# Background matmuls of an attention stream, placed one at a time instead of two

## The chip, the core and the metric

The kernel runs on one core of a Trainium2 chip. The time is the device time in microseconds (us) of one execution; a run is repeated and the median is given. The engines are named as in the profile: PE is TensorE (its matmuls), PEld its weight loads, DVE is VectorE, ACT is ScalarE, POOL is GpSimd, SP is SyncE, which issues the DMAs here. Each engine works through its own queue in order, so an instruction that waits holds up everything behind it on that engine.

## The reference

Two transformer layers with the same weights: attention with 32 heads of 16 columns over 2048 tokens, then a dense layer with SiLU. Matrices are bfloat16.

```
def _A_ref(x, wqkv, wo):            # x: 2048 x 512, 32 heads of 16
    q, k, v = split_heads(x @ wqkv)
    p = softmax(q k^T / 4)          # 32 x 2048 x 2048
    return merge_heads(p @ v) @ wo
def _B_ref(x, w1, w2):              # 512 -> 1792 -> 512
    return silu(x @ w1) @ w2
for layer in range(2):
    x = x + _A_ref(layernorm(x), wqkv, wo)
    x = x + _B_ref(layernorm(x), w1, w2)
```

## The kernel before

**The stream.** The 2048 x 2048 scores of 32 heads and two layers are cut into blocks of 128 keys by 512 queries for one head: 4096 blocks. A batch (`t` in the main loop) holds four blocks. PE makes their scores in one group, since each score has only 32 contraction rows and four of them fit the array side by side (`score`, L852). ACT exponentiates three of the four blocks, in one instruction of 512 columns and one of 1024 (`exp`, L1083). DVE makes the fourth by writing the bits of a half-precision number directly (`emit_d`, `d_y`, L1001), and POOL derives two more terms of it (`d_z`). In every second batch, called a pv batch below (`t in pv_steps`), PE multiplies the exponentials of two batches with the values (`emit_pv`, `to_o`, L876). There are 1024 batches. The first ones, before the DVE path has started, give ACT all four blocks.

**The background.** Everything else of both layers is cut into parts and put between the batches: the projections to queries, keys, values and output (`proj_q`, `proj_k`, `proj_v`, `out_add`, all through `mm4`: four matmuls of 128 x 128 by 128 x 512 into one PSUM bank), the two dense products (`ffn`: `h_ps` by `mm4`, 14 times per block of 512 tokens, each followed by a tanh on ACT and a product on DVE, then four sums of 14 matmuls each in `f_ps`), the layer norms (`xn`), and the normalization of the heads (`rec`, `attn`, L601 and L603). A background product takes its PSUM bank from the pool `m`, which has one buffer once the first batches are over. The next group's first matmul therefore waits until DVE has read the last group out.

**The order** is fixed when the program is built. `Model` keeps an estimate of the time at which PE, ACT and DVE are done, and `part(...)` announces what the next piece of a background generator costs: `pe` for time on PE, `dve` for time on DVE. After the scores, values and exponentials of a batch are emitted, the main loop asks `bg.heads(t)` for candidates and takes one as long as `bg.fits(item)` says yes. For PE, `fits` wants the piece, the next scores and their way to ACT, and a margin of 0.1 us, to end before ACT's queue runs out:

```
        if pe:
            end = self.pe_end(pe, sums) + self.SWITCH
            return end + self.GROUP + self.TO_ACT + self.margin <= self.act
```

`SWITCH` (0.1 us) is charged when PE goes from one kind of matmul to another, `GROUP` (0.217 us) for a matmul of 512 columns or a group of four small ones side by side. When a result is needed at once, `bg.ensure` places its pieces without asking. When no background of PE was placed in a batch that is not a pv batch, `fill` adds three groups of multiplications with zeros, to keep PE busy. After the last batch what is left is emitted, and `tail` does the last block's output projection and dense layer on its own.

Of the kernel before, what the change touches and what calls it, by code (L numbers as in the profile page):

```python
# [24 lines left out]
def part(dve=0.0, pe=0.0, held=False, sums=False, need=None):  # L25

    return Part(held, pe, dve, sums, need)
# [191 lines left out]
def kernel(  # L219
# [19 lines left out]
    CT = D // P  # L239
    NC = S // 512  # L240
    FT = F // P
# [70 lines left out]
    def load_x(c, src=None, parts=1):  # L312
        x_sb[c] = xpool.tile([P, 4, D], BF16, name="x", tag="x")
        if src is None:
            src = xf[512 * c : 512 * (c + 1), :].rearrange("(tt p) d -> p tt d", p=P)
        n = 4 // parts
        for i in range(0, 4, n):
            nc.sync.dma_start(x_sb[c][:, i : i + n, :], src[:, i : i + n, :])
# [26 lines left out]
    bg = Background()  # L345
# [35 lines left out]
    def bank(name, dtype=FP32):  # L381
        home = "o" if early[0] and next(turn) % 2 else "m"
        shape = [P, 2048 // mybir.dt.size(dtype)]
        return psum[home].tile(shape, dtype, name=name, tag=home)[:]
# [34 lines left out]
    def ln_pair(c, i):  # L419

        stats[c, i] = yield from ln_stats(c, (i, i + 1))
# [26 lines left out]
    def ln_attn(L, c):  # L448
        xnT[L, c] = xslot((c, (c + 1) % 4)[L], "xnT")
        if L == 0 and c + 1 < NC:  # L450
            load_x(c + 1)
        yield from ln_chunk(c, xnT[L, c])
        if L == 0 and c + 1 == NC:
            load_x(0)
# [4 lines left out]

    def mm4(name, lhs, rhs, out=0.6):  # L460

        yield part(pe=0.43)
        ps = bank(name)
        for ct in range(CT):
            r = rhs(ct)
            nc.tensor.matmul(  # L466
                ps.rearrange("p (t q) -> p t q", q=P) if len(r.shape) == 3 else ps,
                lhsT=lhs(ct),
                rhs=r,
                start=(ct == 0),  # L470
                stop=(ct == CT - 1),
            )
            if ct == 1:
                yield part(pe=0.43, held=True)
        yield part(out, held=True)
        return ps

# [151 lines left out]
    def load_wo():  # L629

        wo[0] = hpool.tile([P, FT, 512], BF16, name="wo", tag="hT")
        nc.sync.dma_start(wo[0][:, 0:CT, :], A_wo.rearrange("(ct p) e -> p ct e", p=P))
# [15 lines left out]
    def silu_tanh(h_ps, t_sb):  # L648
        nc.scalar.activation(t_sb, h_ps, ACT.Tanh, scale=0.5)  # L649

    def silu_mul(ft, h_ps, t_sb, hT):
        nc.vector.scalar_tensor_tensor(  # L652
            out=hT[:, ft, :], in0=t_sb, scalar=1.0, in1=h_ps, op0=ALU.add, op1=ALU.mult
        )

    def ffn_out(L, c, i, y_ps):
        nc.vector.scalar_tensor_tensor(
            out=x_sb[c][:, i, :],
            in0=y_ps,
            scalar=0.5,  # L660
            in1=x_sb[c][:, i, :],
            op0=ALU.mult,
            op1=ALU.add,
        )
        tt = 4 * c + i
        nc.sync.dma_start(of[tt * P : (tt + 1) * P, :] if L == 1 else x1[c][:, i, :], x_sb[c][:, i, :])
# [23 lines left out]
    def ffn(L, c):  # L690
        if (L, c) != (1, NC - 1):
            nxt = (c + 1) % NC
            load_x(nxt, x1[nxt] if (L, c) >= (0, NC - 1) else None)
        w1 = W1()
        yield part(need=("fT", L, c))
        fT = fTs.pop((L, c))
        hT = hpool.tile([P, FT, 512], BF16, name="hT", tag="hT")
        for ft in range(FT):
            w = w1.get(ft)
            h_ps = yield from mm4(  # L700
                "h_ps", lambda ct: w[:, ct, :], lambda ct: fT[:, :, ct, :], out=0
            )
            t_sb = tpool.tile([P, 512], FP32, name="t_sb", tag="t")
            silu_tanh(h_ps, t_sb[:])
            yield part(0.6, held=True)
            silu_mul(ft, h_ps, t_sb[:], hT)
        for tq in range(4):
            yield part(pe=0.43)
            y_ps = bank("f_ps")
            for ft in range(FT):  # L710
                nc.tensor.matmul(  # L711
                    y_ps,
                    lhsT=hT[:, ft, tq * P : (tq + 1) * P],
                    rhs=w2_sb[:, ft, :],
                    start=(ft == 0),
                    stop=(ft == FT - 1),
                )
                if ft % 2 == 1 and ft < FT - 1:
                    yield part(pe=0.43, held=True)
            yield part(0.6, held=True)  # L720
            ffn_out(L, c, tq, y_ps)
            if L == 0 and tq % 2 == 1:
                bg.add_side(None, ln_pair(c, tq - 1))
        if L == 0:
            bg.add_side(("ln", 1, c), ln_attn(1, c))
        if (L, c) != (1, NC - 1):
            load_wo()
# [98 lines left out]
    steps, pv_steps = plan()  # L826
    pv_left = {}
    for ts in pv_steps.values():
        t, k = ts[0]
# [19 lines left out]
    def score(blk, out):  # L849
        L, qc, pi, g, par, kt, j = blk  # L850
        r = slice(32 * j, 32 * j + 32)
        nc.tensor.matmul(  # L852
            out,
            lhsT=KT[L, kt // 4][r, g, (kt % 4) * P : (kt % 4 + 1) * P],
            rhs=QT[g][r, par, :],
            start=True,
            stop=True,
        )
# [187 lines left out]
    with tc.manual_schedule(  # L1046
# [47 lines left out]
        def score_pair():  # L1094
            return psum["s"].tile([P, 2, 512], FP32, name="s_ps", tag="s2", bufs=2)
# [13 lines left out]
        for t in range(1, len(steps)):  # L1109
            a_blks, d_blks = steps[t]  # L1110
            for L, qc, pi, g, par, kt, j in a_blks + d_blks:
                bg.ensure(q_of[L, qc, pi, g, par])
                if qc == 0:
                    bg.ensure(("k", L, kt // 4, g))
            L, qc, pi, g, par, kt, j = a_blks[0]
            if kt == kts_of[L, qc, pi, g, par][0]:
                for Lq, c, gq, n in q_next.get((L, qc, pi, g, par), []):
                    bg.add(("q", Lq, c, gq, n), proj_q(Lq, c, gq), first=True)
            s2 = score_pair()[:]
            n1 = len(a_blks) - 2  # L1120
            s1 = [
                psum["s"].tile([P, 512], FP32, name="s1_ps", tag=tag, bufs=1)[:]
                for tag in ("s1", "sd")[0:n1]
            ]
            for i in range(2):
                score(a_blks[n1 + i], s2[:, i, :])
            for i in range(n1):
                score(a_blks[i], s1[i])
            if n1 == 1:
                for blk in d_blks:  # L1130
                    emit_d(t, blk)
            m.scores(len(a_blks), len(d_blks))
            while after:
                after.pop()()
                m.sums()
            if t in pv_steps:
                m.pv(emit_pv(t, pv_step(t)))
            if t < D_LEAD:
                p = p_pre[:, 3 * t + 1 : 3 * t + 4, :]
                parts = [p[:, 0:n1, :], p[:, n1 : n1 + 2, :]]  # L1140
            elif n1 == 1:
                p = ppool.tile([P, 3, 512], BF16, name="p_sb", tag="p")
                parts = [p[:, 0:1, :], p[:, 1:3, :]]
            else:
                parts = [
                    dpool.tile([P, 2, 512], U16, name="p_z", tag=f"z{k}")[:].bitcast(BF16)
                    for k in range(2)
                ]
            p_tiles[t] = [p[:, i, :] for p in parts for i in range(p.shape[1])]
            for i in range(n1):  # L1150
                exp(p_tiles[t][i], s1[i])
            exp(flat(parts[1]), flat(s2))
            m.exps(len(a_blks))
            if t <= 4:
                bg.ensure(("v", 0, 0, t - 1))
            if t == 5:
                early[0] = m.early = False
            busy = t in pv_steps
            late = L == 0 or qc == 0
            while True:  # L1160
                for item in bg.heads(t):
                    if bg.fits(item) and (late or not item[2].pe or item[2].sums or t not in pv_steps):
                        break
                else:
                    break
                busy = busy or item[2].pe > 0
                bg.advance(item)
            if n1 == 2 and d_blks:
                m.late_d()
                emit_d(t, d_blks[0])  # L1170
            if not busy and m.fill_fits(FILL):
                n = fill(FILL)
                if n:
                    m.pv(n)
        t = len(steps) + 1
# [38 lines left out]
```

The softmax here doesn't subtract the row's maximum and nothing guards it: scores larger than these inputs give would overflow.

## Time and profile before

| | |
|---|---|
| time, median of 3 runs | 1571.72 us (1569.5 to 1572.07) |
| span of the profiled execution | 1564.6 us |
| first exponential of the stream | 13.95 us |
| last exponential of the stream ends | 1520.46 us |
| stretch after the stream | 44.1 us |
| PE clock granted at half speed | 32.6 to 46.2, 87.2 to 90.6, 967.8 to 971.3 and 1203.4 to 1206.8 us |

The page lists, for each engine, its busy time and share of the span, then the chain of work that ended last, then groups of instructions by source line. A group's row gives the busy time, the mean duration of one instruction, and the idle time of the engine just before such instructions with what ended it. A duration on ACT runs from its first read to its last write, and instructions on ACT overlap; what one of them costs is read from the distance between the ends of two neighbours. Matmuls overlap in the same way.

### The profile page before, as it was taken

The numbers are of one execution on the slowest core, as the hardware profiler recorded it, in microseconds if no ns is written. First come the engines' busy times: TensorE is split into PE (matmuls) and PEld (weight loads), VectorE is DVE, ScalarE is ACT, GpSimd is POOL, SyncE is SP. The second block draws the span as 40 slices with busy tenths as digits, with TensorE's granted clock in tenths as the row PEclk, the third lists the DMA queues.
The fourth block names the chain that finished last, engine by engine and source line by source line (L and its number), as shares of the span: only waits on it lengthen the run. The fifth ranks groups of instructions, "written<-read, shape, count | busy, mean of one in ns | idle before, by whom it ended". The sixth has DMA issues, their size and how long they took to land.

```text
span 1564.6 us, 34115 instructions
## 1 busy us (share of the span) xinstructions
PE 1467.7 (94%) x13311; PEld 460.2 (29%) x13311; DVE 1078.8 (69%) x1719; ACT 1511.7 (97%) x2177; POOL 1114.0 (71%) x1172
## 2 busy tenths in 40 slices
PE   7999998899989999899998999998999899989998
PEld 3222332232222322222222323322332232222223
DVE  6877677667766777667776667676677666766644
ACT  6999999999999999999999999999999999999982
POOL 2888777677876788677876777776777677776750
PEclk9999999999999999999999999999999999999999
DMA  4110013111121102201021010121012110120102
GB/s 140 30 28 2 5 38 62 31 32 28 45 48 25 36 21 55 49 18 44 16 52 41 8 34 10 23 62 32 21 42 61 29 31 15 45 51 22 28 15 51
DMA packets 154193, 55.82 MB, mean 36 GB/s; under 512 B 134064, under 2 KB 153520, under 8 KB 154032
## 3 DMA queue, kind: packets, MB, share of 16 engines
q1 hardware_dynamic: 154032, 53.65, 14.1%
q8 instruction: 104, 1.70, 0.4%
q14 instruction: 57, 0.47, 0.1%
HBM read 28.57 MB, written 4.19 MB: 21 GB/s over the span
## 4 chain that ended last, share of the span: by engine, by line
ACT 82%; PE 9%; DVE 4%; issue 3%; DMA 1%; POOL 1%; SPq 0%; DVEq 0%
ACT p_sb L1083 79%; ACT t_sb L649 3%; PE o_ps L876 3%; PE s_ps L852 2%; DVE d_y L1001 1%; PE h_ps L466 1%; PE f_ps L770 1%; PE d_ps L852 1%; DVE st L392 1%; DVE attn L603 1%; DVE xn L402 1%; SPq L517 0%; PE q_ps L466 0%; PE k_ps L466 0%; ACT p_pre L1083 0%
## 5 line engine op out<-in xcount | busy, mean ns | idle before, releaser
L1083 ACT ACTIVATE p_sb<-s_ps 128x512 bf16<-128x512 f32 x2026 | 1467.0, 1102 | 7.3 <-PE d_ps L852 6.1
L1001 DVE TENSOR_SCALAR d_y<-d_ps 128x512 uint16<-128x512 f32 x1012 | 696.9, 689 | 404.1 <-PE d_ps L852 360.9
L852 PE MATMUL s_ps<-QT,KT 32*128 32x512 bf16 x3084 | 630.6, 383 | 59.4 <-ACT p_sb L1083 44.9
L852 PE MATMUL d_ps<-QT,KT 32*128 32x512 bf16 x1012 | 390.1, 385 | 8.4 <-DVE d_y L1001 5.2
L852 PEld LDWEIGHTS <-KT 32*128 32x128 bf16 x4096 | 187.0, 91 | 647.3 <-issue 595.2
L876 PE MATMUL o_ps<-p_sb,VA 128*32 128x512 bf16 x3039 | 312.4, 389 | 8.2 <-DVE oB L981 1.1
L876 PE MATMUL o_ps<-d_y,VA 128*32 128x512 f16 x1012 | 153.4, 380 | 0.0
L876 PEld LDWEIGHTS <-VA 128*32 128x32 bf16 x4096 | 86.7, 95 | 160.0 <-issue 122.2
L711 PE MATMUL f_ps<-w_sb,hT 128*128 128x512 bf16 x392 | 104.0, 382 | 0.0
L876 PEld LDWEIGHTS <-VB 128*32 128x32 f16 x2024 | 78.4, 98 | 55.6 <-issue 0.8
L876 PE MATMUL o_ps<-w_qkv,zero 128*32 128x512 bf16 x1344 | 93.1, 383 | 0.0
L649 ACT ACTIVATE t_sb<-h_ps 128x512 f32<-128x512 f32 x98 | 86.5, 882 | 0.0
L652 DVE SCALAR_TENSOR_TENSOR hT<-t_sb,h_ps 128x512 bf16<-128x512 f32 x98 | 67.3, 686 | 22.6 <-ACT t_sb L649 22.3
L603 DVE TENSOR_TENSOR attn<-ot,rec 128x256 bf16<-128x256 bf16 x45 | 49.6, 1102 | 1.5
L981 DVE CAST oT<-o_ps 128x512 bf16<-128x512 f32 x64 | 43.5, 680 | 7.7 <-PE o_ps L876 7.7
L402 DVE TENSOR_SCALAR xn<-x,mv,rstd 128x512 bf16<-128x512 bf16 x64 | 42.6, 679 | 3.3 <-POOL rstd L397 1.8
L392 DVE BATCH_NORM_STATS2 st<-x 128x6 f32<-128x512 bf16 x64 | 43.5, 680 | 1.8 <-DMA x<-in_A_x_dram 1.8
L711 PEld LDWEIGHTS <-hT 128*128 128x128 bf16 x392 | 29.2, 97 | 46.4 <-issue 25.0
L876 PEld LDWEIGHTS <-zero 128*32 128x32 bf16 x1344 | 25.5, 95 | 40.2 <-issue 28.0
L466 PE MATMUL k_ps<-xnT,w_qkv 128*128 128x512 bf16 x128 | 35.4, 390 | 1.0 <-DVE xnT L431 0.9
L466 PE MATMUL q_ps<-xnT,w_qkv 128*128 128x512 bf16 x136 | 35.7, 382 | 0.0
L466 PE MATMUL v_ps<-w_qkv,xnT 128*128 128x512 bf16 x128 | 34.7, 382 | 0.1
(2319 smaller groups left out, 2057.4 us busy)
## 6 DMA issues: line engine op xcount, KB each, us to landing
wo<-in_A_wo_dram SPq DMA_DIRECT2D x8, 512.0 KB, 3.7
QT<-q SPq DMA_DIRECT2D x240, 16.0 KB, 1.8
x<-in_A_x_dram SPq DMA_DIRECT2D x7, 512.0 KB, 4.3
out_dram<-x SPq DMA_DIRECT2D x16, 128.0 KB, 1.7
w_sb<-in_B_w_dram SPq DMA_DIRECT2D x1, 1792.0 KB, 14.0
w_qkv<-in_A_wqkv_dram SPq DMA_DIRECT2D x3, 512.0 KB, 7.4
ot<-oT SPq DMA_TRANSPOSE x45, 2.3
x<-in_A_x_dram SPq DMA_DIRECT2D x2, 256.0 KB, 2.9
```

The source lines that it names most:

```text
L392: nc.vector.bn_stats(st[:], x_sb[c][:, i, :])
L402: nc.vector.tensor_scalar(out=xn[:], in0=x_sb[c][:, i, :], scalar1=mv[:, 0:1], scalar2=rstd, op0=ALU.subtract, op1=ALU.mult,)
L466: nc.tensor.matmul(ps.rearrange("p (t q) -> p t q", q=P) if len(r.shape) == 3 else ps, lhsT=lhs(ct), rhs=r, start=(ct == 0), stop=(ct == C ...
L603: nc.vector.tensor_tensor(out=attn[L, qc][:, :, P * g : P * (g + 1)].rearrange("p t (j s) -> p t j s", s=32)[:, :, :, 16 * par : 16 * par ...
L649: nc.scalar.activation(t_sb, h_ps, ACT.Tanh, scale=0.5)
L652: nc.vector.scalar_tensor_tensor(out=hT[:, ft, :], in0=t_sb, scalar=1.0, in1=h_ps, op0=ALU.add, op1=ALU.mult)
L711: nc.tensor.matmul(y_ps, lhsT=hT[:, ft, tq * P : (tq + 1) * P], rhs=w2_sb[:, ft, :], start=(ft == 0), stop=(ft == FT - 1),)
L852: nc.tensor.matmul(out, lhsT=KT[L, kt // 4][r, g, (kt % 4) * P : (kt % 4 + 1) * P], rhs=QT[g][r, par, :], start=True, stop=True,)
L876: nc.tensor.matmul(o_tiles[key][32 * j : 32 * j + 32, :], lhsT=lhsT, rhs=rhs, start=(o_count[key][j] == 0), stop=stop,)
L981: nc.vector.tensor_copy(out=o, in_=o_tiles[key][:])
L1001: nc.vector.tensor_scalar(out=pr["y"][:, len(pr["ds"]), :], in0=s_ps[:], scalar1=float(1024 * SCALE * math.log2(math.e)), scalar2=float(10 ...
L1083: nc.scalar.activation(p_sb, s_ps, ACT.Exp, bias=-SHIFT * math.log(2.0) + math.log(EXP_SUM), scale=float(SCALE),)
```

## The change

A background product announces its matmuls one by one: `mm4` yields a piece of 0.217 us before each of its four matmuls rather than one of 0.43 us before each pair, and the second dense product does the same with its 14. The condition that kept ordinary background matmuls out of pv batches in layer 1 after its first block of queries (`late`) is removed, so that whatever fits goes into any batch. The purpose is to use gaps on PE that are too short for two matmuls. What is computed and the number of background matmuls stay as they are.

```
     def mm4(name, lhs, rhs, out=0.6):
-        yield part(pe=0.43)
+        yield part(pe=0.217)
         ps = bank(name)
         for ct in range(CT):
...
-            if ct == 1:
-                yield part(pe=0.43, held=True)
+            if ct < CT - 1:
+                yield part(pe=0.217, held=True)
         yield part(out, held=True)
...
         for tq in range(4):
-            yield part(pe=0.43)
+            yield part(pe=0.217)
             y_ps = bank("f_ps")
...
-                if ft % 2 == 1 and ft < FT - 1:
-                    yield part(pe=0.43, held=True)
+                if ft < FT - 1:
+                    yield part(pe=0.217, held=True)
...
             busy = t in pv_steps
-            late = L == 0 or qc == 0
             while True:
                 for item in bg.heads(t):
-                    if bg.fits(item) and (late or not item[2].pe or item[2].sums or t not in pv_steps):
+                    if bg.fits(item):
                         break
```

## The prediction
> **What bounds the kernel now.** I read the page from the top: busy times, then the chain, then the groups.
>
> ```profile
> PE 1467.7 (94%) x13311; PEld 460.2 (29%) x13311; DVE 1078.8 (69%) x1719; ACT 1511.7 (97%) x2177; POOL 1114.0 (71%) x1172
> ACT 82%; PE 9%; DVE 4%; issue 3%; DMA 1%; POOL 1%; SPq 0%; DVEq 0%
> L1083 ACT ACTIVATE p_sb<-s_ps 128x512 bf16<-128x512 f32 x2026 | 1467.0, 1102 | 7.3 <-PE d_ps L852 6.1
> L876 PE MATMUL o_ps<-w_qkv,zero 128*32 128x512 bf16 x1344 | 93.1, 383 | 0.0
> ```
>
> ACT is busy 97% and is 82% of the chain. PE's 94% is not a second bound: 1344 of its matmuls multiply by zeros, put in only to keep it busy. The chain in order of time gives ACT's pace:
>
> ```profile
> 303.82 44.11 ACT p_sb L1083 x63
> ```
>
> That is 32 exponentials of 512 columns and 31 of 1024. The distances between ends in the trace are 0.490 and 0.917 us, and 32 x 0.490 + 31 x 0.917 = 44.1: ACT runs without a gap, 1.407 us a batch. A tanh costs 0.490 too.
>
> All of ACT's stream: 1032 exponentials of 512 columns and 98 tanh, 1130 x 0.490 = 553.7 us; 1026 of 1024 columns, 940.8 us; together 1494.5. From 13.95 to 1520.46 us are 1506.5, so about 12 us of the stream are not ACT's work. Nothing that a placement changes can bring more than these. The waits of ACT and PE say where they are:
>
> ```profile
> ACT p_sb L1083 <- PE d_ps L852: 6.1, 10, 1.2
> ACT p_z L1083 <- PE s_ps L852: 1.9, 5, 0.9
> ```
>
> ```profile
> PE s_ps L852 <- ACT p_sb L1083: 44.9, 108, 0.5
> PE h_ps L466 <- DVE hT L652: 6.5, 6, 1.4
> PE d_ps L852 <- DVE d_y L1001: 5.2, 9, 1.5
> ```
>
> The columns are total, times and longest. PE waits for ACT 108 times, which is free; ACT waits for PE in a few places only. Where one end on ACT comes later after the last than 0.490 or 0.917, I added the excess: 0.3 us at the start (16 us), 4.4 in batches 10 to 17 (32 to 47 us), 1.8 in batches 45 to 47 (87 to 91 us), 1.5 in 159 to 161 (249 to 253 us), 3.4 in five places where a dense layer has just begun (batches 170, 298, 426, 706, 810), 0.9 in crumbs. Sum 12.3.
>
> **What the Trainium skill says.** "TensorE: Matmul & The Clock Gate", Part 1, says that PE falls to half its clock after a window of about 3.4 us with too little work and comes back after a busy one. The trace agrees: PE is at half clock from 32.6 to 46.2 us, and three times for 3.4 us. "TensorEngine Tiling (Array Packing)", Key Properties, says that a change of tiling mode drains the array. The trace shows the price: four `h_ps` matmuls start at 459.15 and the next scores at 460.12 us; at 0.215 us each the four take 0.86, so the change costs 0.11. "SBUF — State Buffer", Who interferes with whom, says that a VectorE instruction with two SBUF inputs is blocked while GpSimd reads SBUF. It agrees: `attn<-ot,rec` (two inputs in SBUF) has a median of 1.275 us, `attn<-att,rec` (one in PSUM) 0.424. The planner prices both at 0.43, and this is what stands behind the five places above.
>
> **The change, part by part.** It removes and adds no needed work: the same matmuls on the same engines, 0 us. I compared the order of instructions of both programs.
>
> *Smaller pieces.* 662 background pieces on PE become 1298, the batches with such a piece go from 388 to 506, and the pv batches among them from 2 to 165. Five matmuls, at times six, are placed over a pair of batches; before there were at most four. Cost on PE for a pair with five: scores 2 x 0.217, values 3 x 0.217, background 5 x 0.217, five mode changes of 0.105: 2.70 us against 2 x 1.407 = 2.81 on ACT. It fits, since ACT is slower than the planner believes (0.48 + 0.905 = 1.385 us). A sixth makes 2.92 and is paid from PE's lead, or hidden by a tanh (0.49). So there is no loss per batch; price 0, hidden under the exponentials.
>
> *Earlier ends.* Each dense layer in the stream is done 7 to 12 batches earlier. Nothing waits for it: the next layer's blocks are needed later, and what is left after the last batch is the same single piece. Worth 0. Fill groups rise from 336 to 438, at 4 matmuls each, also in idle time of PE.
>
> *Batches 5 to 17.* Before, the query product stood whole in batch 8 and PE had no background from 9 to 14; it waited for DVE, the clock fell, and 4.4 us were lost. Now one of its matmuls is in batch 8, three are in 10 and three of the next key product in 12. This is work in the hole. Bounds: all 4.4 us come back, if the clock stays up, or 6 x 0.215 = 1.3 us more are lost, if they run at half clock in a batch where PE is late. I take half: −2.2.
>
> *Batches 45 to 47.* The first wait (1.05 us) comes from DVE, where two `xn` before `d_y` took 2.36 us; it stays. The other 0.7 us is two matmuls of a key product at half clock; they now stand earlier. −0.7.
>
> *Batches 153 to 161.* The fourth `xn` waited 1.24 us for the transposing DMA of the first, and `d_y` and the scores stood behind it. The first `xn` is now in batch 153 rather than 155, so its buffer should be free: −1.5.
>
> *The five starts of a dense layer.* The slow `attn`, then the product that frees bank `m`, then the first `h_ps` matmul, which blocks the queue of PE; the next scores are behind it, and ACT behind them. In both programs these groups start one batch after the slow `attn`, so the wait stays. Behind the blocked matmul stood one more, now two: five times 0.215, +1.1.
>
> *New waits for bank `m`.* Groups that start one batch after the bank's last read go from 146 to 228, of 265. Groups that start two batches after a slow `attn` or `xn` go from 7 to 17. None of the seven before shows a late exponential, so I price the new ones at 0; upper bound 10 x 0.66, the middle of the five losses above.
>
> Sum: −2.2 − 0.7 − 1.5 + 1.1 = −3.3, so 1571.7 − 3.3 = 1568.4 us.
>
> **The rivals.** *Hidden anyway:* the start gains nothing, since there it is DVE that is full (27.4 to 35.2 us nearly without a gap), and a chance stall eats the rest: −0.7 − 1.5 + 1.1 = −1.1, 1570.6. For it: the 44.9 us that PE waited for ACT show that PE's timing rarely matters. Against it: PE, not ACT, was at half clock in the costliest stretch.
>
> *Slower:* PE runs with less lead. Before, it waited for ACT about 0.42 us in each pair of a dense layer, and this absorbed a late DVE; with five matmuls 0.11 us are left. Then the ten new starts cost 0.3 to 0.66 each (3.0 to 6.6), the six matmuls at half clock 1.3, the five starts 1.1, less 1.5 at batch 161: +3.9 to +7.5, so some 1577. For it: DVE's slow instructions are priced at a third. Against it: no such loss in the seven like cases.
>
> *Much faster:* the start and batches 45 to 161 are all clean, and so are the crumbs: −4.4 − 1.8 − 1.5 − 0.9 = −8.6, 1563. It needs the clock to hold everywhere, though DVE's delays remain.
>
> **How the numbers follow.** Forecast with its neighbours down to 1566: 0.38. Hidden: 0.30. Slower: 0.24. Much faster: 0.08. Faster by over 0.2% (below 1568.6) is forecast and much faster, 0.46. The range takes in most of the slower case and leaves out its end, and the end of the much faster one: 1564 to 1577.
>
> **What would show it.** Right: ends on ACT at 0.490 and 0.917 us throughout; late exponentials in batches 10 to 17 well under 4.4 us with a shorter stretch of half clock; none at 161; the five starts of a dense layer still there, at 0.5 to 0.9 us each. Wrong: `h_ps`, `f_ps` or `k_ps` waiting for DVE in many more places, ACT waiting for `s_ps` by 0.1 us in many batches of the dense layers, or new stretches of half clock. A stretch after the stream other than 44 us would be a cause I have not thought of.

## The result, and the profile after

The change makes the kernel slower: 1584.68 us (median of 4, 1580.33 to 1586.07) against 1570.61 of before beside it (4 runs). The ratio is 1.0089, with a 95% interval of 1.006 to 1.0117. The forecast was 1568.4, and its range ended at 1577.

The page of the changed kernel, in the order in which before was read (busy times, chain, groups):

```profile
PE 1457.0 (92%) x13642; PEld 453.8 (29%) x13719; DVE 1070.7 (68%) x1719; ACT 1514.9 (96%) x2177; POOL 1114.6 (71%) x1172
ACT 58%; PE 24%; DVE 10%; issue 3%; DMA 3%; POOL 2%; DVEq 0%; POOLq 0%
L1083 ACT ACTIVATE p_sb<-s_ps 128x512 bf16<-128x512 f32 x2026 | 1465.9, 1040 | 15.6 <-PE d_ps L852 10.3
L876 PE MATMUL o_ps<-w_qkv,zero 128*32 128x512 bf16 x1752 | 122.8, 386 | 0.0
```

ACT has the same 2177 instructions, and their ends still lie 0.490 and 0.917 us apart. But its share of the chain falls from 82% to 58%, with PE and DVE at 24% and 10%: far more often the last thing waited for is a chain from DVE over PE to ACT. ACT's idle time before exponentials doubles, from 7.3 to 15.6 us. The waits (engine, line, waited for: total, times, longest):

```profile
PE s_ps L852 <- ACT p_sb L1083: 50.3, 124, 0.5
PE d_ps L852 <- DVE d_y L1001: 12.7, 29, 2.6
ACT p_sb L1083 <- PE d_ps L852: 10.3, 28, 1.0
ACT p_sb L1083 <- PE s_ps L852: 4.3, 3, 2.2
```

PE waits for `d_y` 29 times rather than 9, and ACT for `d_ps` 28 times rather than 10. The wait for bank `m`, which the prediction watched, grows less: `h_ps` waits for `hT` 7.0 us, before 6.5. Waits of `v_ps` and `k_ps` for this bank are new, 4.4 us in ten places, but late exponentials follow only three of them, 0.56 us in all (batches 235, 363 and 491).

The excess of each end on ACT over 0.490 or 0.917 us, called late time below, is the ledger for all kernels here:

| late time, us | batches 0 to 59 | 60 to 163 | 164 to the end | sum | after the stream |
|---|---|---|---|---|---|
| before | 6.4 | 1.5 | 4.3 | 12.2 | 44.2 |
| changed | 8.3 | 3.9 | 12.6 | 24.7 | 45.7 |

The spans differ by 1578.5 − 1564.6 = 13.9 us: 1.8 + 2.4 + 8.2 in the stream and 1.5 after it, rounded. This profile is of the fastest of the four runs; that of before is of a fast one too (1566.6 us). In the four, 1580.3, 1583.6, 1585.8 and 1586.1 us go with granted clocks of 0.990, 0.987, 0.985 and 0.982.

Here is one of the new small losses, in the second dense product of the first block, from the timeline of the changed kernel (start, duration, engine, instruction, and idle time with its releaser):

```profile
317.04 1.28 DVE L603 TENSOR_TENSOR attn<-ot,rec 128x256 bf16<-128x256 bf16 x1
317.30 1.04 PE L711 MATMUL f_ps<-w_sb,hT 128*128 128x512 bf16 x4
...
318.24 0.68 DVE L1001 TENSOR_SCALAR d_y<-d_ps 128x512 uint16<-128x512 f32 x1
318.27 0.48 PE L852 MATMUL s_ps<-QT,KT 32*128 32x512 bf16 x3
318.97 0.37 PE L852 MATMUL d_ps<-QT,KT 32*128 32x512 bf16 x1 [0.22 <-DVE d_y L1001]
...
320.04 0.39 PE L711 MATMUL f_ps<-w_sb,hT 128*128 128x512 bf16 x1
...
320.36 0.39 PE L852 MATMUL s_ps<-QT,KT 32*128 32x512 bf16 x3
...
320.83 0.60 ACT L1083 ACTIVATE p_sb<-s_ps 128x512 bf16<-128x512 f32 x1 [0.17 <-PE d_ps L852]
```

The slow `attn` holds DVE for 1.28 us where the planner counts 0.43, so `d_y` comes late and the next `d_ps` waits on PE for it. Here one `f_ps` matmul stands in the pv batch (320.04), which with its mode change takes 0.32 us ahead of the next scores (320.36), and the exponential after them is 0.28 us late. The same place in the trace of before has the same slow `attn`, but no matmul of the background in the pv batch and two `f_ps` matmuls rather than four behind the `attn`, and ACT runs through without a gap:

```profile
309.48 12.62 ACT L1083 ACTIVATE p_sb<-s_ps 128x1024 bf16<-128x1024 f32 x17
...
312.72 1.28 DVE L603 TENSOR_TENSOR attn<-ot,rec 128x256 bf16<-128x256 bf16 x1
...
314.65 0.37 PE L852 MATMUL d_ps<-QT,KT 32*128 32x512 bf16 x1
```

Not all of the new losses look like this one. Here the late exponentials from batch 164 on are sorted by what PE waited for just ahead of them, and by whether a background matmul stood in a pv batch just before:

| late time from batch 164, us | before | changed |
|---|---|---|
| `h_ps` waits for `hT` at the start of a dense layer | 3.4 | 4.0 |
| a background matmul stands in a pv batch just before | 0 | 4.2 |
| `d_y` is late, no such matmul | 0.5 | 2.9 |
| the rest (a transfer is late, or the clock is at half) | 0.4 | 1.5 |

So the picture above accounts for at most 4.2 of the 8.2 us. An example of the third row is batch 223, from the timeline of the changed kernel:

```profile
348.55 1.71 DVE L402 TENSOR_SCALAR xn<-x,mv,rstd 128x512 bf16<-128x512 bf16 x2
...
350.91 0.37 PE L852 MATMUL d_ps<-QT,KT 32*128 32x512 bf16 x1 [0.71 <-DVE d_y L1001]
...
352.44 1.51 ACT L1083 ACTIVATE p_sb<-s_ps 128x512 bf16<-128x512 f32 x2 [0.34 <-PE d_ps L852]
```

Here the three pv batches before hold only values. DVE has three layer norms close together, 1.15 us and then 1.71 for two, where before the same three took 0.62 and 1.53 and ACT ran on. The new order of the background has moved them; whether PE also had less lead when they came, the trace does not tell.

### The profile page after: what moved, and what is told of

Its sections match the earlier page's. It is cut to its first block, busy times and chain, and to the rows that moved or that the text cites. A ratio compares the mean times of both kernels' runs of the same rounds, so it can differ in the third digit from the quotient of the medians.

```text
span 1578.5 us, 34840 instructions
## 1 busy us (share of the span) xinstructions
PE 1457.0 (92%) x13642; PEld 453.8 (29%) x13719; DVE 1070.7 (68%) x1719; ACT 1514.9 (96%) x2177; POOL 1114.6 (71%) x1172
## 4 chain that ended last, share of the span: by engine, by line
ACT 58%; PE 24%; DVE 10%; issue 3%; DMA 3%; POOL 2%; DVEq 0%; POOLq 0%
ACT p_sb L1083 54%; PE o_ps L876 8%; PE s_ps L852 7%; DVE d_y L1001 4%; PE f_ps L711 3%; ACT t_sb L649 3%; DMA ot<-oT 1%; PE d_ps L852 1%; PE h_ps L466 1%; DVE xn L402 1%; PE y_ps L466 1%; DVE st L392 1%; PE f_ps L770 1%; PE q_ps L466 1%; DVE attn L603 1%
## 5 line engine op out<-in xcount | busy, mean ns | idle before, releaser
L1083 ACT ACTIVATE p_sb<-s_ps 128x512 bf16<-128x512 f32 x2026 | 1465.9, 1040 | 15.6 <-PE d_ps L852 10.3
L852 PE MATMUL s_ps<-QT,KT 32*128 32x512 bf16 x3084 | 587.6, 384 | 64.1 <-ACT p_sb L1083 50.3
L852 PE MATMUL d_ps<-QT,KT 32*128 32x512 bf16 x1012 | 389.8, 385 | 15.2 <-DVE d_y L1001 12.7
L852 PEld LDWEIGHTS <-KT 32*128 32x128 bf16 x4096 | 166.6, 91 | 583.9 <-issue 539.2
L876 PE MATMUL o_ps<-w_qkv,zero 128*32 128x512 bf16 x1752 | 122.8, 386 | 0.0
L649 ACT ACTIVATE t_sb<-h_ps 128x512 f32<-128x512 f32 x98 | 82.5, 841 | 0.6 <-PE h_ps L466 0.6
L711 PEld LDWEIGHTS <-hT 128*128 128x128 bf16 x392 | 31.3, 97 | 64.8 <-issue 44.2
L876 PEld LDWEIGHTS <-zero 128*32 128x32 bf16 x1752 | 33.4, 95 | 53.5 <-issue 38.0
L603 DVE TENSOR_TENSOR attn<-ot,rec 128x256 bf16<-128x256 bf16 x45 | 41.5, 923 | 1.5
## 6 DMA issues: line engine op xcount, KB each, us to landing
w_sb<-in_B_w_dram SPq DMA_DIRECT2D x1, 1792.0 KB, 13.7
```

The costliest lines, as they stand in the source:

```text
L603: nc.vector.tensor_tensor(out=attn[L, qc][:, :, P * g : P * (g + 1)].rearrange("p t (j s) -> p t j s", s=32)[:, :, :, 16 * par : 16 * par ...
L711: nc.tensor.matmul(y_ps, lhsT=hT[:, ft, tq * P : (tq + 1) * P], rhs=w2_sb[:, ft, :], start=(ft == 0), stop=(ft == FT - 1),)
L852: nc.tensor.matmul(out, lhsT=KT[L, kt // 4][r, g, (kt % 4) * P : (kt % 4 + 1) * P], rhs=QT[g][r, par, :], start=True, stop=True,)
L876: nc.tensor.matmul(o_tiles[key][32 * j : 32 * j + 32, :], lhsT=lhsT, rhs=rhs, start=(o_count[key][j] == 0), stop=stop,)
L1083: nc.scalar.activation(p_sb, s_ps, ACT.Exp, bias=-SHIFT * math.log(2.0) + math.log(EXP_SUM), scale=float(SCALE),)
```

## The experiments

The theory, called *lead*: a background matmul in a pv batch takes from PE the lead over ACT that absorbed a late DVE. The main rival, *granularity*: single matmuls cost by themselves, through more mode changes. Others concern the start, the clock and a DMA. Late times are those of one profile each; two profiles with the same order of matmuls from batch 164 on gave 12.6 and 19.9 us there (see *Pairs until batch 30*), so a few microseconds between two rows prove nothing by themselves.

| kernel | time, us | before beside it | ratio (95% interval) | late time: 0 to 59, 60 to 163, from 164 |
|---|---|---|---|---|
| no pieces in pv batches | 1580.39 | 1568.40 | 1.0073 (1.0052 to 1.0095) | 14.1, 4.1, 5.5 |
| pairs until batch 30 | 1584.81 | 1568.40 | 1.0108 (1.0086 to 1.0129) | 7.6, 6.3, 19.9 |
| four `xn` buffers | 1583.26 | 1568.40 | 1.0091 (1.0073 to 1.0109) | 8.5, 3.8, 16.0 |
| `attn` priced | 1578.18 | 1568.40 | 1.0067 (1.0047 to 1.0087) | 8.3, 1.5, 12.8 |
| single, old condition kept | 1580.09 | 1568.88 | 1.0076 (1.0055 to 1.0097) | 7.4, 4.9, 10.6 |
| no pv pieces after 60 | 1576.42 | 1568.88 | 1.0049 (1.003 to 1.0067) | 7.4, 5.1, 6.6 |
| before, with zeros in pv batches | 1588.34 | 1568.88 | 1.0126 (1.0109 to 1.0143) | 7.7, 0.4, 24.5 |
| margin of 0.25 us | 1588.09 | 1568.88 | 1.0123 (1.0097 to 1.0149) | 14.9, 5.2, 14.1 |
| `mm4` single only | 1578.34 | 1569.20 | 1.0058 (1.0043 to 1.0073) | 9.6, 3.9, 8.6 |
| `f_ps` single only | 1574.84 | 1569.20 | 1.0033 (1.002 to 1.0046) | 6.2, 1.5, 10.8 |
| before, lag and zeros at the start | 1572.61 | 1569.20 | 1.0027 (1.0017 to 1.0037) | 6.7, 3.3, 4.8 |
| single after 163, none in pv | 1571.38 | 1568.90 | 1.0017 (1.001 to 1.0025) | 6.4, 1.5, 6.5 |

**No pieces in pv batches.** In the changed kernel:

```
-                    if bg.fits(item):
+                    if bg.fits(item) and (not item[2].pe or item[2].sums or t not in pv_steps):
```

> The changed kernel, but no ordinary background matmul of PE may stand in a pv batch, in either layer (172 pieces move to other batches). The profile of the change has 24.7 us of late exponentials in the stream against 12.2 before. Theory lead: a matmul in a pv batch (0.215 us and a mode change of 0.105) takes the lead of PE that absorbed a late DVE. Then the small stalls of 0.2 to 0.45 us in the second half of the dense layers (4.7 us in all) go, and part of those at the starts: late exponentials 17 to 19 us, time 1574 to 1578. Rival granularity: the single matmuls cost by themselves, through more mode changes, wherever they stand: late exponentials stay at 23 or more, time 1581 to 1586.

From batch 164 on late time falls from 12.6 to 5.5 us, as lead said. The totals were a miss: 1580.4 us, and 23.7 us of late time, which is what the rival gave. Batch 37 alone lost 4.9 us. A value product and a key product had come late there: PE waited 3.1 us for POOL to make `VB` from the values, and then the four matmuls of the key product stood in the pv batch, 1.6 us.

**No pv pieces after 60** repairs this by adding `t < 60 or` inside the new bracket.

> The changed kernel without background matmuls in pv batches from batch 60 on; batches 1 to 59 as in the changed kernel. In the run without any, a key product was not ready and had to be placed whole at batch 37, which lost 6 us that have nothing to do with the theory. Theory lead: that loss is gone, the late exponentials after batch 163 are 5 to 6 us rather than 13, in all 16 to 19 us, time 1573 to 1577. Rival: the losses move elsewhere, the sum stays above 22 us and the time above 1579.

The time is in the range of lead, 1576.4 us. Late time is 19.1 us in all and 6.6 from batch 164, each a little above what was given. The ratio is 1.0049 where the change has 1.0089, so about 6 us less, though the matmuls are still placed singly; the two intervals just overlap. This run does not separate lead from mode changes: in the traces PE changes the kind of matmul 2023 times before, 2158 times in the changed kernel, and 2012 times here.

**Before, with zeros in pv batches.** No background piece is made smaller or moved. In the kernel before:

```
+            if t >= 164 and t in pv_steps:
+                fill(2)
             if not busy and m.fill_fits(FILL):
```

> The kernel before, with its order, and two groups of multiplications with zeros more in every pv batch from 164 on (0.43 us of PE, which the planner isn't told of). No background matmul is smaller or moved. Theory lead: PE's lead is spent as in the changed kernel, so the stalls behind a slow attn or xn appear, at least 8 us more of late exponentials after batch 163 (12 or more, from 4.3), time 1576 to 1590. Rival granularity: no such stalls without smaller pieces, within 2 us of before. Rival clock: what costs the time is a PE that idles and falls to half clock; more work on PE keeps the clock up, so at most as slow as before and a granted clock of 0.993 or more.

This run decides between the two. The groups fit into 368 pv batches. With the old pieces, the old order and as many changes of kind as before (2023), 24.5 us are lost from batch 164 on. So neither single matmuls nor more mode changes are needed for such a loss. Its size says nothing of the change's, for the added work is larger: with four background matmuls a pair of batches now takes 11 x 0.217 + 4 x 0.105 = 2.81 us on PE, and ACT's two batches take 2.81. Its timeline around the same `attn` as above:

```profile
313.35 1.28 DVE L603 TENSOR_TENSOR attn<-ot,rec 128x256 bf16<-128x256 bf16 x1
...
315.28 0.37 PE L852 MATMUL d_ps<-QT,KT 32*128 32x512 bf16 x1 [0.26 <-DVE d_y L1001]
...
316.24 0.60 PE L876 MATMUL o_ps<-w_qkv,zero 128*32 128x512 bf16 x8
316.77 0.39 PE L852 MATMUL s_ps<-QT,KT 32*128 32x512 bf16 x3
...
317.24 5.73 ACT L1083 ACTIVATE p_sb<-s_ps 128x512 bf16<-128x512 f32 x8 [0.32 <-PE d_ps L852]
```

The same chain: `attn`, late `d_y`, `d_ps` waiting 0.26 us, then the added work, then ACT idle. The exponential is 0.43 us late, in the same batch (201) in which the change is 0.28 late; so too in 217. The waits of that run:

```profile
ACT p_sb L1083 <- PE d_ps L852: 19.2, 54, 1.8
PE d_ps L852 <- DVE d_y L1001: 10.0, 35, 1.0
PE s_ps L852 <- ACT p_sb L1083: 10.0, 21, 0.5
```

PE's free waiting for ACT, in which its lead shows, fell from 44.9 us in 108 places to 10.0 in 21, and ACT's waiting for PE took its place. In the changed kernel this total did not fall, it rose to 50.3: there lead is spent in single places, and no total shows it. The clock is answered too:

```profile
core 0: 1586.5 us, clock 0.992
```

This is the clock of before, and from batch 164 to the end of the stream PE is never at half clock in this profile. So a loss of this size needs no fall of the clock.

**Single, old condition kept** restores `late` in the changed kernel and keeps the single matmuls.

> One half of the change alone: single matmuls, but the old condition that keeps them out of the pv batches of layer 1 after its first block of queries (117 pieces in pv batches rather than 172). Theory lead: the late exponentials of the changed kernel from batch 690 on (5.5 us) fall to the 2.2 us that the run without pv pieces shows there; the rest stays, so about 3 us under the changed kernel, 1579 to 1583. Rival granularity: nothing moves, 1582 to 1586.

From batch 690 on late time falls from 5.4 to 3.1 us, not quite to 2.2, and the time is inside the range expected. By the ratios, 1.0089 and 1.0076, removing the condition would cost some 2 us and the smaller pieces the rest, but the intervals overlap, so the share of the condition is not shown. With pairs, removing the condition alone leaves the order of instructions as it was: no pair fits there.

**The two halves of the smaller pieces**, each with pairs kept in the other place:

> One half alone: mm4 places single matmuls in all batches, the second dense product keeps its pairs (111 pieces in pv batches, against 172 of the change and 4 before). Theory lead: each half spends lead where it stands, so both halves cost something; here the stalls of 0.28 us at batches 201, 329, 457, 737 and 841 (in the second dense product) are gone and those around the projections and h_ps stay, late exponentials after batch 163 about 9 us rather than 13, and the start as in the change (7 us), time 1579 to 1583. Rival: the first half carries the whole loss, 1583 to 1586.

> The other half alone: the second dense product places single matmuls in all batches, mm4 keeps its pairs (68 pieces in pv batches). Batches 1 to 160 are as before. Theory lead: start and batches 153 to 161 as before (4.4, 1.8 and 1.5 us), the stalls at 201, 329, 457, 737 and 841 as in the changed kernel, late exponentials in all 15 to 18 us, 3 to 6 us slower than before, 1572 to 1575. Rival: the second dense product, whose pieces follow each other without a bank between, has no part in the loss: within 1.5 us of before.

Both cost: +0.58% and +0.33%, together 0.91%, where the whole change has 0.89%. The start is in the first half alone: with `mm4` in pairs batches 9 to 29 lose 4.8 us, with single matmuls 8.3. The losses of 0.28 us at batches 201, 329, 457, 737 and 841 are there to the hundredth in the `f_ps` run (except 457, where a larger one of 1.40 came) and gone in the `mm4` run, as expected. Both totals missed in part: `mm4` came 0.7 us under the range, and `f_ps` at its upper end with 18.5 us of late time where 15 to 18 were expected.

**Margin of 0.25 us** in place of 0.1:

> The changed kernel with a margin of 0.25 rather than 0.1 us that every piece on PE must leave before ACT runs out. 154 of 172 pieces in pv batches stay, the batches with a piece go from 506 to 511. Theory lead: it is the lead and not the number of pieces or their batches that counts; stalls of 0.2 to 0.45 us shrink by 0.15 each or vanish, late exponentials after batch 163 fall from 13 to about 8, time 1577 to 1581. Rival: pieces in pv batches cost as such, no change, 1582 to 1586.

In the single place the theory holds: batches 201, 329, 457 and 737 fall from 0.28 to 0.13 us, by the 0.15 that was added. In the total both it and the rival failed. Work that the margin pushed back collided elsewhere: 14.9 us were lost before batch 60, of them 4.3 in batch 41 behind a DVE that was 3.5 us late.

**`attn` priced** adds `bg.model.dve += 0.8` after each `attn` by DMA.

> The changed kernel, where the planner charges 0.8 us more to DVE after each normalization attn that comes by DMA (1.23 in all, as it takes on the chip, rather than 0.43). Theory lead: the small stalls in the dense layers arise only where the plan spends lead that the slow attn has used already; with the true price the pieces move, the f_ps stalls (4.7 us) and the five at the starts of dense layers (4.0 us) fall to a third, time 1575 to 1579. Rival granularity: the same count of single matmuls and mode changes, so no change (1581 to 1586).

The time is in the range of lead, but not by the way it said. The losses at 201, 329, 457 are gone, as lead says. Those at the starts of dense layers grew from 4.0 to some 6.5 us, because other waits took their place. In the costliest of these, at batch 167 (1.7 us), it is the weights, which stand behind other transfers in SP's queue; the timeline of that run:

```profile
265.36 1.89 PE L466 MATMUL h_ps<-fT,w 128*128 128x512 bf16 x4 [1.58 <-DMA w<-in_B_w_dram]
```

Late time from batch 164 is 12.8, the same as in the change, and the interval of its ratio overlaps that of the change, so no gain is shown.

**Pairs until batch 30** undoes the change at the start alone.

> The changed kernel, with pairs of matmuls as before in batches 1 to 29 and single ones after. Theory start: of the 12.4 us lost, 2.6 are in batches 9 to 29 (7.0 against 4.4 us), because six matmuls of a query and a key product stand there at half clock. Then these batches lose 4.4 us again, late exponentials 22 us, time 2 to 3 us under the changed kernel. Rival chance: the stretch of half clock there moves from run to run and the placement does not matter: no change, or a loss that is as large a little later.

Batches 9 to 29 lose 4.2 us again, as expected, but batch 45 then loses 3.1, and the time is no better (1584.8). In the time the rival held: what is saved at the start was lost again elsewhere. Yet the loss at the start itself is no chance. In the five profiles whose start has pairs and nothing else new (before, this run, the zeros in pv batches, `f_ps` single only, single after 163), batches 9 to 29 lose 4.1 to 4.8 us; in the eight with single matmuls there, 6.6 to 10.3. This profile fell to half clock in thirteen stretches, 58 us in all against 31 of the changed kernel, and lost 19.9 us from batch 164 on, with the same background in each of these batches. So one order can lose 12.6 or 19.9 us there: mostly in the same batches, with larger losses near a fall of the clock.

**Four `xn` buffers**:

```
-    xnpool = ctx.enter_context(tc.tile_pool(name="xnpool", bufs=3))
+    xnpool = ctx.enter_context(tc.tile_pool(name="xnpool", bufs=4))
-    XN_BUFS = 3
+    XN_BUFS = 4
```

> The changed kernel with four buffers for xn rather than three, so that the fourth normalization of a block no longer waits for the transposing DMA of the first. Theory buffer: the 3.9 us lost in batches 161 to 163 come from DVE standing 3.6 us at this wait, with d_y and so the next scores behind it; they fall under 0.5 us, time 3 to 3.5 us under the changed kernel. Rival queue: the transposes stand behind eight q transfers and the loads on SP's queue, so h_ps waits for fT in place of xn for its buffer, and at least 2 us of the loss stay.

The rival held. In the changed kernel DVE waits at this place (first fence); with four buffers PE waits instead (second), and 3.1 of the 3.9 us stay.

```profile
DVE xn L402 <- DMA fT<-xn: 3.6, 1, 3.6
```

```profile
PE h_ps L466 <- DMA fT<-xn: 2.5, 1, 2.5
```

The queue of SP shows why, in the timeline of the changed kernel:

```profile
240.67 5.25 SPq L517 DMA_DIRECT2D QT<-q  x8
245.98 0.57 SPq L318 DMA_DIRECT2D x<-in_A_x_dram  x1
...
247.75 6.72 SPq L308 DMA_TRANSPOSE fT<-xn  x4
```

Eight transfers of a query product, each issued in turn, and three loads stand ahead of the transposes. The first `xn` is ready at 243.7 us, and its transpose is issued at 247.75. The same transfers stood ahead of them in the kernel before; there the first `xn` waited 1.15 us for its turn, here 4.05.

**Single after 163, none in pv.** The order of before up to batch 163, then single matmuls, but not in pv batches.

> The order of the kernel before up to batch 163, then single matmuls, but none in pv batches. Up to five matmuls stand in a batch that is not a pv batch, where before there were four. Theory lead: with start and batches 153 to 161 as before and no piece in a pv batch, what remains of the change is harmless and also useless, since ACT sets the pace: late exponentials after batch 163 of 4 to 6.5 us (before 4.3, and 6.6 in the run without pv pieces after 60), time within 2.5 us of before, 1568 to 1572. Rival granularity: single matmuls cost by themselves, 1573 or more. Rival gain: the finer packing gains once it spends no lead in pv batches, 1567 or less.

1571.4 us, 2.5 over before: inside the limit, at its edge. Without the pieces in pv batches the single matmuls cost some 2 us and gain nothing. The run without pv pieces after 60 was 7.5 us over before. It differs from this one mainly in what stands before batch 164, and its stretch after the stream is 1.6 us longer in the profile, so the change before batch 164 costs up to 5 us.

**Before, lag and zeros at the start** was an attempt at a better kernel: `m.lag = 0.8` is added to the time at which the next bank comes free after an `attn` by DMA, and `fill(2)` stands in batches 9 to 14, where it finds room for its groups in three (9, 12 and 13).

> The kernel before with two additions that spend no lead. The planner expects the bank that DVE frees after a normalization attn by DMA 0.8 us later, so that in the five places the first h_ps matmul moves one pair of batches back; and two groups of zeros stand in each of the pv batches 9 to 14, where PE waits for DVE. If the five losses (3.4 us) come from the blocked h_ps matmul, they fall to under 0.5 us, 2.9 us gained. If the loss of 4.4 us in batches 10 to 17 comes from the half clock, it falls to about 2.5 and the stretch from 32.6 us is shorter or gone; if it comes from DVE being full, it stays. In all 1564 to 1568 where before is about 1569. Rival: DVE is late anyway, the losses only move by a pair of batches: no difference above 1 us.

The five places fall from 3.4 to 1.0 us, not under 0.5 as expected but enough to name the blocked `h_ps` as the main cause. The stretch of half clock at the start shrinks from 13.7 to 6.8 us, but batches 10 to 17 still lose 3.9 of 4.4. This speaks for DVE rather than the clock; it is not proof, since the stretch is not gone. Other batches lose more, 161 above all, and the kernel is 0.27% slower than before, where a gain was expected. Nothing tried here beats before.

## Why the prediction was wrong

*ACT sets the pace and its work stays the same*: right. The ends lie 0.490 and 0.917 us apart in all profiles, and nothing could gain more than 12 us.

*Smaller pieces, price 0, hidden under the exponentials*: this step failed, and it is the largest part of the error. Its sum was right: a pair of batches with five matmuls fits (2.70 in 2.81 us). But it compared sums over a pair, as if what the fifth matmul took were idle time to give away. The idle time of PE in a pv batch was the reserve against a DVE that is late at known places, such as a normalization of 1.28 us priced at 0.43. From batch 164 on the change lost 8.2 us more, where the forecast had +1.1. Of these, 4.2 us at most fall behind a background matmul in a pv batch, and taking these pieces out after batch 60 wins about 6 us of the 14 by the medians. Another 2.4 us fall behind layer norms on DVE that the new order has moved, a term that the prediction does not have; how far lead plays a part there is open. The slower rival said that "PE runs with less lead" and had a chance of 0.24. It then priced the loss at starts that wait for bank `m` (3.0 to 6.6 us). Ten new waits for the bank did come, but 0.56 us of late time follows them, while `d_ps` waiting for `d_y` rose from 5.2 to 12.7 us.

*The five starts of a dense layer, +1.1*: 4.0 us against 3.4, so +0.6. Right in direction and place.

*Batches 5 to 17, −2.2*: failed. Batches 9 to 29 lost 7.0 rather than 4.4 us. The stated bound the other way (+1.3, six matmuls at half clock) was too small as well: the losses, 1.09, 1.96, 1.0, 0.66 and 0.49 us in batches 12 to 18, fall in the half-clock stretch, which now begins at 36.8 us. *Batches 45 to 47, −0.7*: the number came true, 1.76 became 0.95, but in part by luck: the first wait, which was to stay, fell from 1.05 to 0.66. In other profiles with the old order here the place loses 1.1 to 2.6 us.

*Batches 153 to 161, −1.5*: failed. "Its buffer should be free" took the time at which `xn` is made for the time at which its transpose can start. The transposes stood behind the query transfers and the loads in SP's queue; they started 0.6 us later against ACT than before, and the second took 2.13 rather than 1.20 us. The place lost 3.9 rather than 1.5 us.

*The stretch after the stream*: 45.7 against 44.2 us. The profile has half clock there for 3.4 us from 1545.5. Over all fourteen profiles, this stretch takes 45.5 to 46.2 us in the ten that have half clock in it, two of them with the old pieces, and 44.2 in the four that have none, three of them with single matmuls. So the 1.5 us go with the clock, and the change is neither needed for it nor enough. Still open: why `rec` waits for its transposed input 6.4 us in the change and 0.7 before.

## What to carry to other kernels

Idle time on an engine that feeds the bound engine is not all free: part of it is the reserve that absorbs late inputs, and a filler that uses it can turn small delays behind it into time of the bound engine. Before pricing such work at zero, look for the longest delays that the slack now swallows (here a normalization that takes three times its planned time) and compare them with the slack that will remain at that place, not on average. Ask, too, what else a new order of the filler moves, on other engines as well. And a buffer made ready earlier helps only if the queue of the transfer that empties it is free by then.

## What the hardware showed that was not expected

Extra PE work of 0.43 us in 368 pv batches cost 19.5 us in all, with the mean clock of before (0.992). The change's own runs scatter with the clock: 1580.3 us at 0.990, 1586.1 at 0.982. A late scores group leaves PE idle, and where the clock then falls to half, the following batches are late too: in the changed kernel the clock is halved for 3.4 us from 255.2 us, as the loss of 2.36 us in batch 161 ends, and the next batch loses another 1.09.
